# Scores of heads 4, 5, 8 and 9 as one float32 product instead of two FP32R products

## The chip, the cores and the metric

One NeuronCore of a Trainium2 chip runs the whole program. The metric is device time in microseconds of one execution, the median over several runs; a profile records one execution in full.

## The reference

Sparse attention, then two dense stages. Shapes: 2 batches, 8 heads, sequence 768, head dimension 64; so there are 16 heads in all, counted 0 to 15 below (head i is head i mod 8 of batch i div 8).

```
scores = q @ k.T / 8                      # per batch and head, 768 x 768
keep   = (key < 8) or (0 <= query - key < 96)
scores = where(keep, scores - slope[h] * distance, -1e9)
a      = softmax(scores); attn = a @ v    # slope[h] = 2 ** -(h + 1)
x      = attn, heads side by side         # 2 x 768 x 512
theta  = x @ w_theta
u      = x + w_tok_r @ (x * cos(theta)) + w_tok_i @ (x * sin(theta))
x2     = u + relu(u @ w_ch)
h      = relu(x2 @ w_in); c = conv3(h); out = (h * sigmoid(c)) @ w_out
```

All tensors are float32, the weights of the dense stages float64 bits that the kernel converts.

## The kernel before, in words

**Row tiles and steps.** A head is cut into six tiles of 128 query rows. Each tile needs only 232 key columns (96 before it, the 8 global ones, its own 128; tile 0 only its own 128). Two tiles are one step: step j = 3i + tp is part tp (0, 1, 2) of head i, and `run_fast` (L879) is one loop over all 48 steps and the lags behind them. In step j it emits, in this order: the scores of step j (`scores`, L353), the row minima of step j-1 on VectorE (`softmax`, L380), the exponentials of j-2 on ScalarE (`exps`, L395), the transposes of j-3 on TensorE (`transposes`, L402), their copy from PSUM of j-4 on ScalarE (`evacuate`, L412), the product with V of j-5 (`pv`, L416), and for every third step the normalisation of a head on VectorE (`normalise`, L291). The order of this loop is the order of each engine's instructions; there is no other scheduler.

**Scores.** The step's PSUM bank first takes a bias product (the "table" against a scaled identity, `eye`, written by POOL in `slope`, L333); heads 10 and later drop that product in their second and third step and add the bias on VectorE instead (`fused`, L344). Then come the tiles' products, L377. There are two ways:
- *Split*, heads 2 to 15: float32 is split into a high part in FP32R and a low rest. K holds the high part of the keys on partitions 0 to 63 and the low part on 64 to 127; Q is there twice, so that one FP32R product gives q_high * (k_high + k_low) and a second one q_low * (k_high + k_low). The parts are made in `split` (L264): query high by ScalarE (L306, `"  A"`), query low by VectorE (L310, `"   V"`), key low by VectorE (L90, `" V"`). The high key part is loaded directly by a POOL DMA (`keys`, L261) into K of buffer i mod 2, which it can enter only when the scores of head i-2 have been computed. Queries (128 x 768) and the keys' lower copy (64 x 816) come by two SP DMAs into a staging buffer (`load`, L249).
- *Whole*, heads 0 and 1: one float32 product of unsplit operands, L367. Queries of head 0 stand on partitions 0 to 63 of `scratch`, those of head 1 on 64 to 127 of the first columns of `xs[1]`, zeros on the other half; the keys of both heads stand one above the other in `scratch`, so that the zeros leave out the other head's keys. The queries are scaled in place by ScalarE.

For head i+1 the split is emitted during head i: query high in its first step, the two low parts in its second, followed by `load(i + 3)`; `keys(i + 2)` stands in the third step of head i, `load_v(i + 1)` too.

**Between the heads.** When two heads of a batch are done, their 128 columns of x are transposed (`transpose_x`, L526) in two groups of three on TensorE (tile X, a single PSUM bank), one group in the first and one in the second step of heads 4, 6, 8 and so on; ScalarE copies each group out (tile xT), the first copy in the same step as the second group. `split_xT` (L537) on VectorE follows in the next head. The theta products of batch 0 run from about head 11 on among the steps.

**The conveyor.** The float64 weights are converted piece by piece by `Net.conveyor` (L148): per piece six steps, `magnitude` (ScalarE, L98), three bit operations on VectorE (L102, L106, L110; the last frees the staging buffer and lets SP load the next piece), the high part (ScalarE, L82) and the low part (VectorE, L90). `net.run(k)` (L183) makes k steps of it; the last line of the loop says how many per step. Twelve pieces belong to this stage; what is left of them is finished after the loop (`tail`, L748).

Of the kernel before, what the change touches and what calls it, by code (L numbers as in the profile page):

```python
# [19 lines left out]
B, H, S, D = 2, 8, 768, 64  # L20
DM, DFF = H * D, 1024
P = 128
# [3 lines left out]
NH = B * H  # L26
# [10 lines left out]
STAGE = S + NT * KW  # L37
# [3 lines left out]
TURN = 6.283185  # L41
TWO32 = float(2.0 ** 32)
FUSED = 10
LAG_SM, LAG_EXP, LAG_T, LAG_EV, LAG_PV, LAG_N = 1, 2, 3, 4, 5, 6


# [178 lines left out]
class Attention:  # L225
# [21 lines left out]
        self.xs = xs  # L247

    def load(self, i, whole=False):  # L249
        if i < NH:  # L250
            b, h = divmod(i, H)
            src, st = self.net.io["qk"][b, :, h, :], self.st[i % 2]
            if whole:
                self.nc.sync.dma_start(st, src)
            else:
                self.nc.sync.dma_start(st[:, 0:S], src[:, 0:S])
                self.nc.sync.dma_start(st[D:P, S:STAGE], src[D:P, S:STAGE])

    def keys(self, i):
        if i < NH:  # L260
            b, h = divmod(i, H)  # L261
            self.nc.gpsimd.dma_start(self.K(i), self.net.io["qk"][b, :, h, S:STAGE])

# [39 lines left out]
def scaled(net, eh, el, q, hi, lo):  # L303
    nc = net.nc
    if eh == "A":
        nc.scalar.activation(hi, q, AF.Copy, scale=QSCALE)  # L306
    elif eh == "V":
        nc.vector.tensor_scalar(hi, q, QSCALE, None, op0=ALU.mult)
    if el == "V":
        nc.vector.scalar_tensor_tensor(lo, q, QSCALE, hi.bitcast(F32), op0=ALU.mult, op1=ALU.subtract)  # L310


class FastAttention(Attention):
# [6 lines left out]
        self.o = {}  # L320
        self.whole = [net.head["scratch"][:, 0:S], xs[1].rearrange("p t d -> p (t d)")[:, 0:S]]

    def second(self):

        nc, q = self.nc, self.whole[1]
        nc.sync.dma_start(q[D:P], self.net.io["qk"][0, D:P, 1, 0:S])
        nc.gpsimd.memset(q[0:D], 0.0)

    def eye(self, i):
        h = i % H  # L330
# [7 lines left out]
    def spread(self, i):  # L338

        if FUSED <= i < NH:  # L340
            T = self.net.head["table"][:, RW:].bitcast(F32)
            self.nc.gpsimd.tensor_scalar(self.bias[i % 2], T, 2.0 ** -(i % H + 1), None, op0=ALU.mult)

    def fused(self, j):  # L344
        return j % 3 > 0 and j // 3 >= FUSED

# [6 lines left out]
    def scores(self, j):  # L353

        i, tp = divmod(j, 3)
        net = self.net
        Q, K, T = self.Q(i), self.K(i), net.head["table"]
        sp = net.bank("TH", 1) if tp == 2 and i < NH // 2 + 2 else net.bank("S", 2)
        f = self.fused(j)
        if tp == 0:  # L360
            net.mm(sp[:, 0 : 2 * RW], self.eye(i), T, True, False)
        elif not f:
            net.mm(
                sp[:, 0 : 2 * RW].rearrange("p (u c) -> p u c", u=2), self.eye(i),
                T[:, RW:].unsqueeze(1).to_broadcast([P, 2, RW]), True, False,
            )
        if i < 2:  # L367
            Q, K = self.whole[i].unsqueeze(1), net.head["scratch"][:, S:STAGE]
        A = Q.shape[1]
        for u in range(2):  # L370
            t = 2 * tp + u
            if t == 0:
                o, r = sp[:, PG:RW], K[:, 0:P]
            else:
                o, r = sp[:, RW * u : RW * u + RW], K[:, KW * (t - 1) + SKIP : KW * t + P]
            for a in range(A):
                net.mm(o, Q[:, a, t * P : t * P + P], r, f and a == 0, a == 1 if f else u + a == A)  # L377
        self.state[j] = {"sp": sp}
# [100 lines left out]
class Mix:  # L479
# [46 lines left out]
    def transpose_x(self, b, c, e="AA", second="X"):  # L526

        n = self.net
        for hf in range(2):
            xb = n.bank(second, 2) if hf and second != "X" else n.bank("X")  # L530
            for jj in range(3):
                t = 3 * hf + jj
                self.nc.tensor.transpose(xb[:, P * jj : P * jj + P], self.xs[b][:, t, P * c : P * c + P], n.head["ident"])
            yield
            n.hi(e[hf], self.xT[b][:, c, HALF * hf : HALF * hf + HALF], xb[:, 0:HALF])
# [343 lines left out]
def run_fast(tc, net):  # L879
    nc, io = net.nc, net.io  # L880
    xs = [net.slot(f"xs{b}", [P, NT, DM], F32, "xs") for b in range(2)]
    att = FastAttention(net, xs)
    mix = Mix(net, xs)
    att.slope(0)
    att.second()
    att.keys(2)
    att.load_v(0)
    att.load(2)
    att.load_v(1)
    att.load(3)  # L890
    mix.begin()
    mix.alloc_xTs()
    NJ = 3 * NH
    OPEN = {
        NJ + 2: ((0, (0, 1)),), NJ + 3: ((1, (0, 1)),), NJ + 4: ((2, (0, 1)),),
        NJ + 6: ((0, (2,)), (1, (2,)), (2, (2,)), (3, (0, 1, 2))),
    }
    first, last, splits, theta0 = Pipe(), Pipe(), deque(), None

    def theta_0():  # L900
        for t in range(NT):
            tiles = mix.theta(t, "TH", 1)
            for k in range(2):
                for _ in range(6):
                    th = next(tiles)
                yield
            first.add(later(mix.reduce_theta(th, mix.r[:, t])))

    def later(g):
        next(g)  # L910
        yield
        yield
        next(g, None)

    early = mix.trig0()

    def split(b, c):
        for _ in range(3 if (b, c) in ((0, 3), (1, 2)) else 5):
            yield
        splits.append((b, c))  # L920

    for j in range(NJ + LAG_N + 3):
        i, tp = divmod(j, 3)
        if j < NJ:
            att.scores(j)
        first.step()
        if 0 <= j - LAG_SM < NJ:
            att.softmax(j - LAG_SM)
        if tp == 1 and i + 1 < NH and (i + 1 < 3 or (i + 1) % H > 2):
            att.slope(i + 1)  # L930
        if tp == 1:
            att.spread(i + 1)
        if 0 <= j - LAG_EXP < NJ:
            att.exps(j - LAG_EXP)
        if 0 <= j - LAG_T < NJ:
            att.transposes(j - LAG_T)
        if 0 <= j - LAG_EV < NJ:
            att.evacuate(j - LAG_EV)
        if 0 <= j - LAG_PV < NJ:
            att.pv(j - LAG_PV)  # L940
        jj = j - LAG_N
        if 0 <= jj < NJ and jj % 3 == 2:
            att.normalise(jj // 3, att.o.pop(jj // 3))
        if j == 0:
            scaled(net, "A", None, att.whole[1][D:P], att.whole[1][D:P], None)
        if tp == 2:
            if i != 1:
                att.keys(i + 2 if i else 3)
        elif i > 0 and tp == 0:
            att.split(i + 1, "  A")  # L950
        elif i > 0:
            att.split(i + 1, "   V")
            att.split(i + 1, " V")
            att.load(i + 3)
        if i > 0 and tp == 2 and i + 1 < NH:
            att.load_v(i + 1)
        last.step()
        jj = j - LAG_N - 1
        if jj == NJ - 1:
            for chain in (mix.transpose_x(1, KC - 1, "AV", "O"), mix.split_xT(1, KC - 1, "V")):  # L960
                for _ in chain:
                    pass
        elif 0 <= jj < NJ and jj % 6 == 5:
            bc = divmod(jj // 6, KC)
            last.add(mix.transpose_x(*bc), split(*bc))
        if splits and (splits[0][0] == 0 or theta0 == "done"):
            b, c = splits.popleft()
            last.add(mix.split_xT(b, c, "V"))
            if (b, c) == (0, KC - 1):
                theta0 = theta_0()  # L970
        elif theta0 and theta0 != "done" and next(theta0, last) is last:
            theta0 = "done"
            mix.alloc_xTs()
        for t, cs in OPEN.get(j, ()):
            mix.theta1(t, cs)
        if NJ + 4 <= j <= NJ + 6:
            next(early, None)
        if j == 3:
            net.fetch()
        if 6 < j < NJ + 3:  # L980
            net.run(2 if j >= NJ else (3, 2, 3)[tp] if i > 10 else (2, 1, 1)[tp] if i % 2 else (1, 0, 1)[tp])
    last.drain()
    mix.tail(early)

# [44 lines left out]
def build(nc, io):  # L1029
    with tile.TileContext(nc) as tc, tc.tile_pool(name="const", bufs=1) as small:  # L1030
        head = {}
        net = Net(tc, io, small, None, None, head)
        with tc.tile_pool(name="idle", bufs=1, space=bass.MemoryType.PSUM) as ps, tc.manual_schedule():
            begin(nc, io, net, small, head, ps.tile([P, 512], F32, name="idle"))
        rv = nc.values_load(
            head["flag"][:1, :1], min_val=0, max_val=1, skip_runtime_bounds_check_because="it is the product of comparisons, 0 or 1"
        )
        with tc.If(rv == 1) as cmp:
            arm(tc, io, head, run_fast)
        with cmp.Else():  # L1040
            arm(tc, io, head, run_general)
# [95 lines left out]
```

## Time and profile before

| what | value |
|---|---|
| median of 3 runs | 424.14 us (423.72 to 425.51) |
| the profiled execution | 422.92 us, span 421.0 us |
| TensorE busy | 405.9 us, 96% |
| VectorE busy | 332.9 us, 79% |
| ScalarE busy | 223.9 us, 53% |
| GpSimd (POOL) busy | 23.8 us, 6% |
| read from memory, written | 42.99 MB, 3.15 MB |

The span is the time from the first to the last instruction of the profiled execution; the execution's own time holds some 2 us more around it. In the rows below PE is TensorE, PEld its weight loads, DVE VectorE, ACT ScalarE, POOL GpSimd, SP the queue that issues most DMAs. A row of a timeline gives the start, the duration, the engine, the line, the operation, output and inputs by name, shapes and count, and in brackets the idle time before it with what ended it. A matmul's end is modelled, so the distance between two starts says more than a duration. A float32 product shows as two matmul records, an FP32R product as one.

### The profile page before, as it was taken

The numbers are of one execution on the slowest core, as the hardware profiler recorded it, in microseconds if no ns is written. First come the engines' busy times: TensorE is split into PE (matmuls) and PEld (weight loads), VectorE is DVE, ScalarE is ACT, GpSimd is POOL, SyncE is SP. The second block draws the span as 40 slices with busy tenths as digits, with TensorE's granted clock in tenths as the row PEclk, the third lists the DMA queues.
The fourth block names the chain that finished last, engine by engine and source line by source line (L and its number), as shares of the span: only waits on it lengthen the run. The fifth ranks groups of instructions, "written<-read, shape, count | busy, mean of one in ns | idle before, by whom it ended". The sixth has DMA issues, their size and how long they took to land.

```text
span 421.0 us, 6542 instructions
## 1 busy us (share of the span) xinstructions
PE 405.9 (96%) x2418; PEld 379.4 (90%) x2418; DVE 332.9 (79%) x619; ACT 223.9 (53%) x443; POOL 23.8 (6%) x45
## 2 busy tenths in 40 slices
PE   8979989999999999999999999999999999999994
PEld 4969879889998899999999999999999998888884
DVE  5768989999868985999989999999999999800000
ACT  4749667868778875824535336455645546200000
POOL 5011103121200000000000000000000000000000
PEclk9998999999999999999999999999999999999999
DMA  5998788786410034025466553131000000110111
GB/s 171 318 259 277 184 256 243 214 224 177 143 39 1 2 113 112 2 75 181 123 198 200 154 149 100 52 100 51 2 0 2 0 0 2 60 54 36 50 51 58
DMA packets 17130, 46.66 MB, mean 111 GB/s; under 512 B 2304, under 2 KB 2752, under 8 KB 17088
## 3 DMA queue, kind: packets, MB, share of 16 engines
q1 hardware_dynamic: 14768, 40.10, 32.2%
q0 software_dynamic: 2016, 5.85, 4.9%
q8 instruction: 21, 0.34, 0.4%
q10 hardware_dynamic: 304, 0.20, 0.2%
q14 instruction: 21, 0.17, 0.1%
HBM read 42.99 MB, written 3.15 MB: 110 GB/s over the span
## 4 chain that ended last, share of the span: by engine, by line
PE 68%; DMA 12%; ACT 8%; DVE 7%; issue 4%; SPq 1%; POOL 0%; DVEq 0%; POOLq 0%; ACTq 0%
PE S L93 17%; PE O L93 17%; PE PT L93 14%; PE TH L93 11%; DMA qk<-qk 8%; PE X L93 7%; DMA a<-qk 2%; DMA wst<-w_tok 1%; DVE qk L90 1%; PE PT L409 1%; ACT a L400 1%; ACT z L82 1%; ACT qk L306 1%; ACT scratch L588 1%; DVE z L90 1%
## 5 line engine op out<-in xcount | busy, mean ns | idle before, releaser
L98 ACT ACTIVATE wbit<-wst 128x512 f32<-128x512 f32 (+1 forms) x38 | 23.4, 617 | 17.5 <-DMA wst<-w_tok 5.9
L93 PE MATMUL O<-a,a 128*128 128x65 f32 x236 | 30.7, 272 | 0.0
L93 PEld LDWEIGHTS O<-a,a 128*128 128x128 f32 x236 | 29.8, 196 | 0.2
L400 ACT ACTIVATE a<-S,nm 128x232 f32<-128x232 f32 (+1 forms) x52 | 19.7, 438 | 16.8 <-DVE rs L296 13.6
L82 ACT ACTIVATE a<-PT 128x512 f32<-128x512 f32 (+1 forms) x48 | 27.5, 572 | 1.2 <-PE PT L409 1.1
L409 PE MATMUL PT<-ident,a 128*128 128x128 f32 x176 | 27.1, 272 | 0.0
L93 PE MATMUL O<-wt,z 128*128 128x384 f32 x144 | 26.9, 334 | 0.0
L93 PE MATMUL TH<-wth,xTs 128*128 128x512 f32 x96 | 26.4, 409 | 0.3 <-ACT scratch L577 0.3
L93 PEld LDWEIGHTS S<-qk 128*128 128x128 f32 x136 | 20.2, 194 | 6.5 <-DVE qk L90 4.2
L93 PE MATMUL PT<-wt,z 128*128 128x384 f32 x132 | 25.8, 335 | 0.0
L93 PE MATMUL S<-qk 128*128 128x232 f32 (+1 forms) x136 | 21.9, 284 | 3.5 <-DVE qk L90 3.4
L93 PEld LDWEIGHTS O<-wt,z 128*128 128x128 f32 x144 | 25.2, 188 | 0.1
L110 DVE SCALAR_TENSOR_TENSOR wbit<-wst,wbit 128x512 int32<-128x512 int32 (+1 forms) x38 | 23.9, 630 | 1.2
L106 DVE SCALAR_TENSOR_TENSOR wbit<-wst,wbit 128x512 int32<-128x512 int32 (+1 forms) x38 | 24.2, 636 | 0.9
L82 ACT ACTIVATE wt<-wbit 128x384 fp32r<-128x384 f32 x24 | 12.6, 526 | 22.0 <-DVE wbit L110 13.5
L93 PEld LDWEIGHTS PT<-wt,z 128*128 128x128 f32 x132 | 23.2, 188 | 0.0
L93 PE MATMUL S<-wt,z 128*128 128x384 f32 x120 | 22.3, 336 | 0.1
L93 PEld LDWEIGHTS S<-wt,z 128*128 128x128 f32 x120 | 20.9, 188 | 0.4 <-ACT scratch L577 0.4
L90 DVE TENSOR_TENSOR qk<-a,qk 64x816 fp32r<-64x816 f32 x14 | 14.1, 1005 | 9.1 <-DMA qk<-qk 8.8
L102 DVE TENSOR_SCALAR wbit<-wbit 128x512 int32<-128x512 int32 (+1 forms) x48 | 18.7, 390 | 3.1 <-ACT wbit L98 3.0
L93 PEld LDWEIGHTS TH<-wth,xTs 128*128 128x128 f32 x96 | 16.9, 189 | 3.9 <-ACT scratch L577 0.5
L409 PEld LDWEIGHTS PT<-ident,a 128*128 128x128 f32 x176 | 19.9, 141 | 0.2
(224 smaller groups left out, 992.5 us busy)
## 6 DMA issues: line engine op xcount, KB each, us to landing
wst<-w_tok SPq DMA_DIRECT2D x18, 384.0 KB, 3.7
a<-v SPq DMA_DIRECT2D x16, 357.5 KB, 5.6
qk<-qk POOLq DMA_DIRECT2D x14, 408.0 KB, 5.7
a<-qk SPq DMA_DIRECT2D x14, 384.0 KB, 3.9
wst<-w_out SPq DMA_DIRECT2D x8, 512.0 KB, 3.6
a<-qk SPq DMA_DIRECT2D x14, 204.0 KB, 5.5
out<-scratch SPq DMA_DIRECT2D x11, 256.0 KB, 2.0
wst<-w_in SPq DMA_DIRECT2D x5, 512.0 KB, 4.0
```

Of the source, the lines that this page charges most:

```text
L82: self.nc.scalar.activation(out, in_, AF.Copy)
L90: e.tensor_tensor(out, in_, hi.bitcast(F32), op=ALU.subtract)
L93: self.nc.tensor.matmul(out, l, r, start=start, stop=stop)
L98: self.nc.scalar.activation(t.bitcast(F32), w[:, 1 : w.shape[1] : 2].bitcast(F32), AF.Copy, scale=REBIAS)
L102: self.nc.vector.tensor_scalar(t, t, 3, None, op0=ALU.logical_shift_left)
L106: self.nc.vector.scalar_tensor_tensor(t, w[:, 0 : w.shape[1] : 2], 29, t, op0=ALU.logical_shift_right, op1=ALU.bitwise_or)
L110: self.nc.vector.scalar_tensor_tensor(t, w[:, 1 : w.shape[1] : 2], -(1 << 31), t, op0=ALU.bitwise_and, op1=ALU.bitwise_or)
L306: nc.scalar.activation(hi, q, AF.Copy, scale=QSCALE)
L400: self.nc.scalar.activation(sS[:, c], x[:, c], AF.Exp, bias=s["nm"][:, u : u + 1], scale=-1.0)
L409: self.nc.tensor.transpose(pt[:, c], sS[:, self.columns(u, a)], net.head["ident"])
L588: nc.scalar.activation(a, a, AF.Sin, bias=n.head["half_pi"], scale=-TURN)
```

## The change

`WHOLE` names the heads that are computed whole: 0, 1, 4, 5, 8 and 9. For these `load`, `keys` and `split` do nothing. `pair(i)`, for i = 4 and 8, brings the queries and keys of heads i and i+1 on SP: queries of head i, the keys of both, queries of head i+1, into the same places that heads 0 and 1 used; it is emitted in the second step of head i-2, after `load`. `scale(i)` scales a query on ScalarE in the second step of the head before. Heads 0 and 1 keep their loads and zeros; head 1's scaling moves from step 0 to step 1. The conveyor's step counts per step of the loop change: from 2, 1, 1 (odd heads) and 1, 0, 1 (even heads) to 2, 2, 2 in heads 3, 4, 7 and 8 and 1, 0, 1 in the other heads up to 10; 3, 2, 3 in heads 11 to 15 stay; the 2 in each of the three steps past the last head go.

```diff
@@ -41,6 +41,7 @@
 TURN = 6.283185
 TWO32 = float(2.0 ** 32)
 FUSED = 10
+WHOLE = (0, 1, 4, 5, 8, 9)
 LAG_SM, LAG_EXP, LAG_T, LAG_EV, LAG_PV, LAG_N = 1, 2, 3, 4, 5, 6
 
 
@@ -247,7 +248,7 @@
         self.xs = xs
 
     def load(self, i, whole=False):
-        if i < NH:
+        if whole or (i < NH and i not in WHOLE):
             b, h = divmod(i, H)
             src, st = self.net.io["qk"][b, :, h, :], self.st[i % 2]
             if whole:
@@ -257,7 +258,7 @@
                 self.nc.sync.dma_start(st[D:P, S:STAGE], src[D:P, S:STAGE])
 
     def keys(self, i):
-        if i < NH:
+        if i < NH and i not in WHOLE:
             b, h = divmod(i, H)
             self.nc.gpsimd.dma_start(self.K(i), self.net.io["qk"][b, :, h, S:STAGE])
 
@@ -320,11 +321,26 @@
         self.o = {}
         self.whole = [net.head["scratch"][:, 0:S], xs[1].rearrange("p t d -> p (t d)")[:, 0:S]]
 
-    def second(self):
-
-        nc, q = self.nc, self.whole[1]
-        nc.sync.dma_start(q[D:P], self.net.io["qk"][0, D:P, 1, 0:S])
-        nc.gpsimd.memset(q[0:D], 0.0)
+    def half(self, i):
+        return slice(D * (i % 2), D * (i % 2) + D)
+
+    def query(self, i):
+        b, h = divmod(i, H)
+        r = self.half(i)
+        self.nc.sync.dma_start(self.whole[i % 2][r], self.net.io["qk"][b, r, h, 0:S])
+
+    def pair(self, i):
+
+        self.query(i)
+        for x in (i, i + 1):
+            b, h = divmod(x, H)
+            r = self.half(x)
+            self.nc.sync.dma_start(self.net.head["scratch"][r, S:STAGE], self.net.io["qk"][b, r, h, S:STAGE])
+        self.query(i + 1)
+
+    def scale(self, i):
+        q = self.whole[i % 2][self.half(i)]
+        scaled(self.net, "A", None, q, q, None)
 
     def eye(self, i):
         h = i % H
@@ -364,8 +380,8 @@
                 sp[:, 0 : 2 * RW].rearrange("p (u c) -> p u c", u=2), self.eye(i),
                 T[:, RW:].unsqueeze(1).to_broadcast([P, 2, RW]), True, False,
             )
-        if i < 2:
-            Q, K = self.whole[i].unsqueeze(1), net.head["scratch"][:, S:STAGE]
+        if i in WHOLE:
+            Q, K = self.whole[i % 2].unsqueeze(1), net.head["scratch"][:, S:STAGE]
         A = Q.shape[1]
         for u in range(2):
             t = 2 * tp + u
@@ -882,7 +898,8 @@
     att = FastAttention(net, xs)
     mix = Mix(net, xs)
     att.slope(0)
-    att.second()
+    att.query(1)
+    nc.gpsimd.memset(att.whole[1][0:D], 0.0)
     att.keys(2)
     att.load_v(0)
     att.load(2)
@@ -941,17 +958,21 @@
         jj = j - LAG_N
         if 0 <= jj < NJ and jj % 3 == 2:
             att.normalise(jj // 3, att.o.pop(jj // 3))
-        if j == 0:
-            scaled(net, "A", None, att.whole[1][D:P], att.whole[1][D:P], None)
         if tp == 2:
             if i != 1:
                 att.keys(i + 2 if i else 3)
-        elif i > 0 and tp == 0:
-            att.split(i + 1, "  A")
-        elif i > 0:
-            att.split(i + 1, "   V")
-            att.split(i + 1, " V")
+        elif i > 0 and i + 1 not in WHOLE:
+            if tp == 0:
+                att.split(i + 1, "  A")
+            else:
+                att.split(i + 1, "   V")
+                att.split(i + 1, " V")
+        elif tp == 1 and i + 1 in WHOLE:
+            att.scale(i + 1)
+        if tp == 1 and i > 0:
             att.load(i + 3)
+            if i + 2 in WHOLE and i % 2 == 0:
+                att.pair(i + 2)
         if i > 0 and tp == 2 and i + 1 < NH:
             att.load_v(i + 1)
         last.step()
@@ -977,8 +998,8 @@
             next(early, None)
         if j == 3:
             net.fetch()
-        if 6 < j < NJ + 3:
-            net.run(2 if j >= NJ else (3, 2, 3)[tp] if i > 10 else (2, 1, 1)[tp] if i % 2 else (1, 0, 1)[tp])
+        if 6 < j < NJ:
+            net.run((3, 2, 3)[tp] if i > 10 else 2 if i in (3, 4, 7, 8) else (1, 0, 1)[tp])
     last.drain()
     mix.tail(early)
 
```

## Rows read from the trace of the kernel before

**Rows 1.** Page: busy us, share of the span, instructions.

```profile
PE 405.9 (96%) x2418; PEld 379.4 (90%) x2418; DVE 332.9 (79%) x619; ACT 223.9 (53%) x443; POOL 23.8 (6%) x45
```

**Rows 2.** Stretches by engine: heads 3, 4, 6, 8, 10, then heads 3 to 10.

```profile
21.16:26.79 5.63, 5.63 (x50) 5.57 (x50) 3.88 (x9) 4.92 (x12) 1.09 (x3) 1.00 1.14 289
26.79:37.74 10.95, 8.07 (x56) 7.71 (x56) 8.29 (x16) 6.30 (x16) 1.10 (x3) 0.84 0.77 236
43.37:51.19 7.82, 6.83 (x56) 6.27 (x56) 7.62 (x15) 5.66 (x14) 1.26 (x3) 1.00 0.67 165
56.82:65.20 8.38, 6.88 (x56) 6.27 (x56) 8.18 (x15) 5.66 (x14) 0.54 (x2) 1.00 0.69 188
70.83:78.64 7.81, 6.56 (x54) 5.93 (x54) 7.46 (x18) 5.91 (x15) 2.00 (x4) 1.00 0.79 214
21.16:78.64 57.48, 50.86 (x408) 48.41 (x408) 48.42 (x91) 41.60 (x99) 9.02 (x16) 0.97 0.84 238
```

**Rows 3.** Timeline of TensorE, head 4: start us, us, instructions, idle before.

```profile
30.12 0.71 PE L93 MATMUL S<-qk 128*128 128x128 f32 x4 [2.88 <-DVE qk L90]
...
35.72 0.50 PE L533 MATMUL X<-ident,xs 128*128 128x128 f32 x3
35.98 0.46 PE L93 MATMUL TH<-table,qk 128*128 128x464 f32 x1
```

**Rows 4.** Timeline of TensorE, heads 0, 1 and 2: scores and what follows.

```profile
8.54 0.95 PE L93 MATMUL S<-scratch 128*128 128x232 f32 x4
9.15 0.54 PE L93 MATMUL TH<-table,qk 128*128 128x464 f32 x1
...
10.52 0.78 PE L93 MATMUL S<-scratch,xs 128*128 128x128 f32 x4
11.14 0.49 PE L409 MATMUL PT<-ident,a 128*128 128x128 f32 x3
...
11.68 0.95 PE L93 MATMUL S<-scratch,xs 128*128 128x232 f32 x4
12.46 0.60 PE L409 MATMUL PT<-ident,a 128*128 128x128 f32 x4
...
15.82 0.60 PE L93 MATMUL S<-qk 128*128 128x128 f32 x4
16.26 0.49 PE L409 MATMUL PT<-ident,a 128*128 128x128 f32 x3
...
17.40 0.46 PE L93 MATMUL S<-table,qk 128*128 128x464 f32 x1
17.69 0.62 PE L93 MATMUL S<-qk 128*128 128x232 f32 x4
18.15 0.60 PE L409 MATMUL PT<-ident,a 128*128 128x128 f32 x4
```

**Rows 5.** Waits of TensorE, 10 to 135 us: total, times, longest.

```profile
PE S L93 <- DVE qk L90: 3.4, 2, 2.9
PE X L533 <- ACT xT L82: 2.8, 4, 0.9
```

**Rows 6.** Chain that ended last, 15 to 80 us: start us, us, what.

```profile
20.60 8.44 DMA qk<-qk
...
37.18 5.51 DMA qk<-qk
```

**Rows 7.** Timeline of VectorE, 8 to 48 us.

```profile
23.03 0.69 DVE L106 SCALAR_TENSOR_TENSOR wbit<-wst,wbit 128x512 int32<-128x512 int32 x1
...
24.19 0.95 DVE L310 SCALAR_TENSOR_TENSOR qk<-a,qk 128x768 fp32r<-128x768 f32 x1
29.06 1.00 DVE L90 TENSOR_TENSOR qk<-a,qk 64x816 fp32r<-64x816 f32 x1 [3.92 <-DMA qk<-qk]
```

**Rows 8.** Timeline of ScalarE, 8 to 48 us.

```profile
22.90 0.85 ACT L306 ACTIVATE qk<-a 128x768 fp32r<-128x768 f32 x1 [0.29 <-DMA a<-qk]
...
31.44 0.80 ACT L400 ACTIVATE a<-S,nm 128x232 f32<-128x232 f32 x2 [4.98 <-DVE rs L296]
```

## The prediction

> **What bounds the kernel now.** I read the busy shares, then busy time head by head, then the waits, the chain that ended last, and the timelines around the waits. TensorE is busy 96% of the span [rows 1], so only what TensorE waits for, or is given to do, can move the end. There are two kinds of head. Head 3 takes 5.63 us with TensorE busy throughout, and heads 2, 5, 7 and 9 take the same within 0.01 us. The even heads, which also carry two groups of X transposes, take 10.95 (head 4), 7.82 (6), 8.38 (8) and 7.81 us (10) [rows 2]. A group of X transposes costs 0.26 us where nothing waits (35.72 to 35.98 [rows 3]), so heads 4, 6 and 8 should take about 6.2 us. Head 10 leaves out two bias products of 0.29 us (17.40 to 17.69 [rows 4]), so 5.6 us. The excess is 4.75 + 1.6 + 2.2 + 2.2 = 10.75 us. TensorE's listed idle time from head 3 to head 10 is only 57.48 - 50.86 = 6.6 us [rows 2]; the rest hides in matmul ends, which are modelled, and in head 4's clock: granted 0.84 on average, that is a stretch at 1.2 instead of 2.4 GHz right after the stall.
>
> The waits name two causes: scores that wait for VectorE's qk (longest 2.9 us, at head 4), and X transposes that wait for ScalarE's xT (4 times, up to 0.9 us) [rows 5]. The chain shows them to be one. Head 4's keys are issued at 20.60 us, when head 2 has left their buffer, and land 8.44 us later [rows 6]; VectorE, which has waited 3.92 us for them, subtracts for 1.00 us [rows 7]; TensorE starts head 4's scores right behind, at 30.12 us, after 2.88 us idle [rows 3]. The same link stands in the chain at heads 6, 8 and 10 (5.51 us of transfer for head 6 [rows 6]). 5.5 + 1.0 us from the end of head i's scores to the start of head i+2's does not fit into the 5.63 us of the head between. VectorE works in order: its wait also delays the row minima queued behind the subtraction, so ScalarE's exponentials, so the xT copies on which the X transposes wait.
>
> **The change part by part.**
>
> *Scores.* For heads 4, 5, 8 and 9 two FP32R products per row tile become one float32 product; both show as two matmul records, so the counts are equal. Head 1 already runs so. From its scores to the next operation it is 0.62 us in a head's first step and 0.78 in the second; head 2 takes 0.44 and 0.46 [rows 4]. The third step is like the second, and the bias product grows by 0.01: 0.18 + 0.33 + 0.33, about +0.85 us per head, **+3.4 us** in all, on the path since TensorE is full there. The lower bound is head 0, where a bias product and no transposes follow: 0.61 us (8.54 to 9.15 [rows 4]), 0.15 more per full step, +1.3 us in all. Here transposes follow, as in head 1, so I take 3.4.
>
> The Trainium skill ("FP8 and Floating Point Precision", TensorE Precision Notes) says that true FP32 makes four passes through the array, which speaks against this change. An estimate by that rule, with one pass for each FP32R product, is 1,288 columns per head times two extra passes at 2.4 GHz: 1.07 us per head, 4.3 us in all, and a sum of -4.7 us for the -5.6 below. Head 1's rows agree with the four passes; it is the split pair of head 2 that stays above its own ideal, so the rows show less extra.
>
> *Conversions.* VectorE loses 0.95 + 1.00 us in each of four heads, 7.8 us [rows 7]. ScalarE's 0.85 us over 128 partitions [rows 8] becomes one over 64, for which I take no gain; but it moves from the first to the second step of the head before, behind that step's evacuation and ahead of the xT copy. Head 1's scaling moves from step 0 to step 1; no other ScalarE work of the loop lies between, so 0.
>
> *Transfers.* A head brought in 128 x 768 queries and 64 x 816 keys on SP and 128 x 816 keys on POOL, 996 KB; it now brings 64 x 768 and 64 x 816, 396 KB, on SP. Four POOL issues go, and with them the loop through the keys' buffer for heads 4 to 11: the buffers of heads 6, 7, 10 and 11 were last read by heads 2, 3, 6 and 7, so their keys can start about two heads earlier. POOL keeps its order; ahead of keys(6) and keys(7) stand only eye products, which wait for scores two heads back. On SP the loads for heads 4 and 5, which waited for VectorE, go; load_v(2) and pair(4) move up behind the first weights. q4 waits for head 0's scores (done by 10.5 us), the two key halves for head 1's (about 14.5). If they land as late as head 4's keys did, 8.44 us, that is 23 us at most for the keys; ScalarE came to q4's place at 22.9 us [rows 8], and head 4's scores are due at 26.8. Behind pair(4) on SP stand load_v(3) and load(6), which are used a head or more later, and the weights' loads, which wait for VectorE as before. pair(8) is issued when head 5's scores end, a whole head before ScalarE scales q8 in head 7. So 0.
>
> *Weights.* The conveyor makes 6 steps each in heads 3, 4, 7 and 8 and 2 each in 5, 6, 9 and 10: 32 for 24. Six steps are one weight; four of them are VectorE's, at up to 0.69 us [rows 7], some 2.4 us a weight. Eight steps cost it 3.3 us against the 7.8 freed. From head 3 to head 10 it was busy 48.4 of 57.5 us [rows 2]; it will be 44 of 52. The load is uneven, since heads 5, 7 and 9 also split xT: there VectorE may hold more than TensorE's 5.6 to 6.5 us. I put 0.5 us for that (0 to 1.5). The six steps past the last head go; TensorE is full there, so 0.
>
> *What is late next.* An X group still needs its predecessor's xT copy, in heads 4 and 8 now behind a 0.85 us scaling. TensorE's step there grows by 0.33 us, which covers part of it: 0.4 us each, and 0.2 in heads 6 and 10, so 1.2 us (bounds 0, and the 2.8 us of [rows 5]).
>
> Sum: -10.75 + 3.4 + 0.5 + 1.2 = **-5.6 us**. The profiled execution took 422.92 us with a span of 421.0; this makes 417.3 and a span of 415.4. The median of the runs lies 1.2 us above that execution, so I predict 418.5 us. By the bounds, -10.75 + 1.3 is -9.4, and -10.75 + 3.4 + 1.5 + 2.8 is -3.05: 414.7 to 421.1 us.
>
> **The rivals.** A change of 0.5% (2.1 us) is about what a measurement of this kernel can tell from none.
>
> *Only head 4's stall goes.* The delays in heads 6 to 10 could be ScalarE's own, with exponentials, evacuations, scaling and weight steps in one queue. Then 4.75 us go and 3.4 come: -1.35, 422.8 us. For it: TensorE's idle time is booked to ScalarE's xT 4 times [rows 5]. Against it: before head 4's second step ScalarE itself stood still 4.98 us for VectorE [rows 8], which waited for the keys; the same order holds before heads 6, 8 and 10.
>
> *The wait moves to the pair's loads.* ScalarE works in order, so a scaling that waits for its query holds the exponentials and evacuations behind it. It decides once q4 lands after 22.9 us or the keys after 26.8. To end slower by 2.1 us it must bring 7.7 us of new stall, 3.9 at each of heads 4 and 8; priced at head 4's present excess, 4.75 each, it gives -5.6 + 9.5 = +3.9, 428.0 us. Against it stand the 3 us of slack of the keys and the 600 KB fewer per head.
>
> *More is gained.* If the X waits vanish and the products cost what head 0 shows: -9.4, 414.7 us.
>
> *The change does not do what it says*: keys(6) and keys(10) could still be held by an older instruction on POOL or reach their buffer no earlier. Heads 6 and 10 would keep their excess, 3.8 less the 0.4 already counted: -5.6 + 3.4 = -2.2, 421.9 us.
>
> **How the numbers follow.** Forecast (-3 to -7.5 us): 0.65. More: 0.08. POOL still holds keys: 0.06, half of it faster. Only head 4's stall goes: 0.13. Pair late: 0.08. So faster 0.76, same 0.16, slower 0.08. The range reaches from a little beyond the forecast, 416.0, to the second case, 422.8, which leaves out about 2 in 10.
>
> **What the profile would show.** Right: head 4 begins at about 26.8 us without an idle row, the granted clock stays at 1.00 from 10 us on, heads 4 and 8 take 7.1 to 7.7 us, heads 5 and 9 about 6.5, head 6 at most 6.6, head 10 at most 6.0; head 10 begins near 67 instead of 70.83 us. The float32 score groups take 0.62 and 0.78 us to the next operation. From 130 us on the work is the same, only earlier. Wrong: ScalarE idle until a transfer into scratch or xs lands, X groups still waiting 0.7 us and more, VectorE full in heads 5 to 9 with TensorE waiting for it, or score groups of 1 us and more.

## The result, and the profile after

The changed kernel takes 416.89 us (415.81 to 419.04, four runs) where the kernel before took 424.32 us beside it (423.72 to 425.51): a ratio of 0.9854, with a 95% interval of 0.981 to 0.9899. That is 7.4 us less by the medians and 6.2 by the ratio; 418.5 us was forecast, inside a range of 416.0 to 422.8. The profiled execution took 416.43 us with a span of 414.5, so 6.5 us less than the profiled execution before on both.

First the page, to be read against [rows 1]:

```profile
PE 404.9 (98%) x2418; PEld 380.0 (92%) x2418; DVE 325.6 (79%) x611; ACT 225.2 (54%) x443; POOL 22.3 (5%) x41
```

TensorE has as many matmuls as before and is busy 98% instead of 96%. VectorE has 8 instructions fewer (the two low parts of four heads), POOL 4 (the key loads of those heads).

Then the stretches of the changed kernel by head: head 3, 4, 5, 6, 7, 8, 9, 10, and heads 3 to 10 together (columns as in [rows 2]).

```profile
22.73:28.36 5.63, 5.63 (x51) 5.56 (x50) 4.81 (x11) 4.95 (x11) 1.09 (x2) 1.00 1.04 224
28.36:35.40 7.04, 7.04 (x57) 6.77 (x56) 5.53 (x12) 5.84 (x14) 1.32 (x3) 1.00 1.05 332
35.40:41.87 6.47, 6.47 (x50) 6.20 (x50) 5.21 (x10) 5.54 (x14) 0.52 (x1) 1.00 0.84 201
41.87:48.07 6.20, 6.20 (x56) 6.13 (x56) 6.07 (x11) 5.33 (x13) 0.56 (x1) 1.00 0.84 222
48.07:53.70 5.63, 5.63 (x51) 5.56 (x50) 4.99 (x12) 5.55 (x14) 1.38 (x3) 1.00 1.11 291
53.70:60.74 7.04, 7.04 (x57) 6.77 (x56) 6.57 (x13) 6.32 (x15) 2.45 (x3) 1.00 0.92 300
60.74:67.21 6.47, 6.47 (x51) 6.20 (x50) 4.96 (x10) 4.82 (x12) 0.00 (x0) 1.00 0.44 116
67.21:72.98 5.77, 5.77 (x54) 5.75 (x54) 5.64 (x14) 4.92 (x13) 0.56 (x1) 1.00 0.51 146
22.73:72.98 50.25, 50.25 (x408) 48.94 (x408) 43.77 (x87) 43.27 (x99) 7.89 (x11) 1.00 0.84 231
```

The second number, TensorE's busy time, equals the first in every row: from head 3 to head 10 TensorE is never idle, and its clock is at 2.4 GHz throughout. These heads take 50.25 us where they took 57.48. The price of the float32 products is read by comparing like with like: head 5 against head 7, 6.47 to 5.63, and head 4 against head 6, 7.04 to 6.20, both 0.84 us.

The keys now come early. In the timeline of POOL, the DMA issues of heads 6 and 10:

```profile
27.80 0.58 POOL L263 DMA_DIRECT2D qk<-qk  x1
...
47.51 0.58 POOL L263 DMA_DIRECT2D qk<-qk  x1 [6.58 <-PE TH L94]
```

Head 6 starts at 41.87 and head 10 at 67.21 us, so their keys are issued 14 and 20 us ahead, where it was 6.2 us before (for head 6, 37.18 us in [rows 6] against its start at 43.37 in [rows 2]).

One wait is new. In the changed kernel's waits of TensorE from 10 to 135 us (total, times, longest), only one is left that is longer than 0.3 us:

```profile
PE TH L94 <- ACT a L416: 1.9, 1, 1.9
```

It is the third step of head 1, at 14.98 us. ScalarE stood still there behind head 2's queries, which landed at 13.4 us instead of 11.8 (its timeline):

```profile
13.40 0.84 ACT L307 ACTIVATE qk<-a 128x768 fp32r<-128x768 f32 x1 [2.39 <-DMA a<-qk]
```

So head 2 starts at 17.10 instead of 15.52 us and head 3 at 22.73 instead of 21.16. The account of the span is: +1.57 in front of head 3, -7.23 in heads 3 to 10, and -0.84 behind them; head 11 takes 8.33 us, before 8.74, and the stretch from head 12's start to the end 333.2 us, before 333.6.

### The profile page after: what moved, and what is told of

It reads as the page before. It is cut to its first block, busy times and chain, and to the rows that moved or that the text cites. A ratio compares the mean times of both kernels' runs of the same rounds, so it can differ in the third digit from the quotient of the medians.

```text
span 414.5 us, 6520 instructions
## 1 busy us (share of the span) xinstructions
PE 404.9 (98%) x2418; PEld 380.0 (92%) x2418; DVE 325.6 (79%) x611; ACT 225.2 (54%) x443; POOL 22.3 (5%) x41
## 4 chain that ended last, share of the span: by engine, by line
PE 82%; ACT 5%; DMA 5%; DVE 5%; issue 1%; SPq 0%; DVEq 0%; ACTq 0%
PE O L94 22%; PE S L94 20%; PE PT L94 14%; PE TH L94 13%; PE X L94 7%; PE PT L425 4%; DMA a<-qk 2%; DMA wst<-w_tok 1%; DMA qk<-qk 1%; PE X L549 1%; ACT z L83 1%; ACT scratch L604 1%; DVE z L91 1%; ACT scratch L602 1%; DMA words<-n 1%
## 5 line engine op out<-in xcount | busy, mean ns | idle before, releaser
L407 DVE TENSOR_REDUCE nm<-S 128x2 f32<-128x464 f32 x26 | 16.6, 638 | 6.9 <-PE S L94 5.0
L94 PE MATMUL O<-x,win 128*128 128x384 f32 x96 | 17.4, 336 | 0.0
L94 PE MATMUL O<-wout,g 128*128 128x512 f32 x72 | 17.1, 390 | 0.0
```

The costliest lines, as they stand in the source:

```text
L94: self.nc.tensor.matmul(out, l, r, start=start, stop=stop)
L407: self.nc.vector.tensor_reduce(s["nm"], s["sp"][:, 0 : 2 * RW].rearrange("p (u c) -> p u c", u=2), axis=AX.X, op=ALU.min)
```

## The experiments

Two questions were open: whether the loop through the keys' buffer was the cause of the gain (and not the lighter VectorE, the fewer transfers or the moved conversions), and whether the new wait belongs to the change. Each time is compared with that of the kernel before, run beside it on the same chip; the runs come from three chips. `after_again` (the same kernel again), `v2_late` (the V load moved), `own_keys` (keys in a place of their own) and `old_steps` (the conveyor's steps) ran on the first; `before_new_steps` (the same edit the other way round), `first_pair` (one pair alone), `q2_first` (head 2's loads first) and `third_buffer` on the second; `before_q2_first`, `q2_q3_first` and `pair_and_buffer` (the mixture) on the third. Between chips the ratios are the better comparison.

### The same kernel again, and the V load moved

> The changed kernel once more, as the measure for the three runs beside it, and to see whether the new 1.9 us wait of head 1's third step (ScalarE behind head 2's queries, which landed at 13.4 us instead of 11.8) comes again. If it belongs to the change (the transfers that moved up ahead of it in time, the third V load above all), the wait is there again, over 1.5 us, and head 2 starts at about 17 us. If it was chance, head 2 starts near 15.5 us. Median near 417 us.

Measured: 417.88 us (415.79 to 419.47) against 423.63 before, ratio 0.9843 (0.9801 to 0.9885). The wait was there again, 1.88 us, as was expected if it belonged to the change; `before_new_steps` below decides otherwise. This time TensorE's clock also fell. The stretch from 15 to 18.5 us of this execution (columns as in [rows 2]; the granted clock is the third number from the end):

```profile
15.00:18.50 3.50, 3.48 (x13) 3.11 (x14) 2.56 (x4) 2.69 (x7) 0.00 (x0) 0.53 1.08 290
```

The same stretch of the changed kernel's first profiled execution:

```profile
15.00:18.50 3.50, 3.50 (x27) 3.38 (x27) 2.83 (x5) 2.86 (x8) 0.00 (x0) 1.00 1.06 257
```

The granted clock is 0.53, almost all of the stretch at 1.2 GHz, against 1.00. The idle time ahead of it is the same, 1.88 and 1.90 us; one execution does half the matmuls (13 against 27), and head 3 starts 1.7 us later.

Then the V load of head 2 moved:

```diff
             att.load(i + 3)
             if i + 2 in WHOLE and i % 2 == 0:
                 att.pair(i + 2)
-        if i > 0 and tp == 2 and i + 1 < NH:
+                if i == 2:
+                    att.load_v(2)
+        if i > 1 and tp == 2 and i + 1 < NH:
             att.load_v(i + 1)
```

> The changed kernel with the V load of head 2 emitted behind the pair's loads of heads 4 and 5, so that it is issued at about 17 us instead of 10.7. If the new wait in head 1 comes from that load sharing the DMA engines with head 2's queries, these land near 11.8 us again, head 2 starts about 1.5 us earlier and the time falls by 1 to 1.5 us against the changed kernel of the same call. If the wait is chance or comes from the queries' own place in the queue, nothing moves by more than 0.5 us.

Measured: 418.08 us (416.15 to 419.64), no faster than the changed kernel. In its profiled execution the wait was gone and head 2 started at 14.99 us, yet the runs gained nothing. The profile shows where it went: head 2 starts 2.1 us earlier than in the changed kernel's first profile and the span is only 0.2 us shorter, because heads 2 and 3 take 12.09 instead of 11.26 us and the stretch behind head 10 takes 342.6 instead of 341.5. So what the start gains can be lost elsewhere, and this median alone does not clear the V load. A later run settles it: the kernel `first_pair` below issues the V load early, at 10.84 us, as the change does, and had no such wait; `before_new_steps` below does not issue it before 17.16 us and had it. So the early V load is neither enough for the wait nor needed for it, and the cause named in the expectation falls.

### The keys in a place of their own, nothing else changed

```diff
+    def K(self, i):
+        if i in (4, 5, 8, 9):
+            x = NT * KW * (i % 2)
+            return self.spare[:, x : x + NT * KW]
+        return self.qk[i % 2][:, 2 * S :]
...
     mix.begin()
+    att.spare = mix.wt[0][1].rearrange("p a b c -> p (a b c)")
```

> The kernel before, with nothing changed but the place of the high keys of heads 4, 5, 8 and 9: they go to an idle FP32R tile instead of the buffer that heads 2, 3, 6 and 7 still read. All conversions, transfers and FP32R products stay. Theory (the loop through the keys' buffer set the pace, and the change gained by breaking it): the 10.75 us of excess in heads 4, 6, 8 and 10 go for the most part without the 3.4 us of float32 products; heads 3 to 10 take 48 to 51 us instead of 57.5, bounded by VectorE, which stays at 48 us busy there; median 413 to 418 us. Rival (the change gained by what it takes off VectorE and the DMA queues): VectorE and the transfers are as full as before, heads 3 to 10 stay at 55 us or more, median 421 us or more.

Measured: 417.85 us, ratio 0.9843 (0.9801 to 0.9884): the same as the changed kernel. Its heads 3 to 10:

```profile
24.76:73.72 48.96, 47.56 (x408) 46.55 (x408) 47.18 (x87) 40.77 (x96) 8.00 (x13) 1.00 0.96 261
```

Its waits of TensorE from 10 to 135 us, the first of them head 1's third step again:

```profile
PE TH L93 <- ACT a L406: 2.2, 1, 2.2
PE X L539 <- ACT xT L82: 1.8, 3, 0.9
```

48.96 us, although every head but 0 and 1 is still split, VectorE still does all its conversions (47.18 us busy, before 48.42) and all transfers remain. So the rival falls, and the loop through the buffer is what the change removed: opening it alone takes 8.5 us off these heads, the change 7.2. The float32 products are one way to open it, and what they save VectorE repays their price of 3.4 us only in part. In heads 4 to 7 they buy nothing: 23.64 us here, 25.34 in the changed kernel, 30.03 before. In heads 8 to 10 they buy a little: 19.69, 19.28 and 21.82 us. What they buy there is visible in the second row: with VectorE nearly full, X groups still wait 1.8 us, 1.3 of them in heads 8 and 10. ScalarE, which copies the groups out, waits 5.5 us for VectorE's `rs` between 25 and 75 us, in the changed kernel 0.5.

Heads 3 to 10 are 1.3 us shorter than in the changed kernel and the time is the same. In this profile the stretch behind head 10 takes 343.0 us, in the changed kernel's two 341.5 and 342.0; 1.1 us of it are two waits of TensorE, 0.66 us for VectorE at 82.33 us and 0.45 us for an X group's copy at 123.22.

### The conveyor's steps

```diff
-        if 6 < j < NJ:
-            net.run((3, 2, 3)[tp] if i > 10 else 2 if i in (3, 4, 7, 8) else (1, 0, 1)[tp])
+        if 6 < j < NJ + 3:
+            net.run(2 if j >= NJ else (3, 2, 3)[tp] if i > 10 else (2, 1, 1)[tp] if i % 2 else (1, 0, 1)[tp])
```

> The changed kernel with the conveyor's steps per loop step as before. Theory: TensorE is full in heads 3 to 10 either way, so those heads take 50.3 us within 0.5, and what the six steps behind the last head cost is at most the 0.45 us that an X group waited there: the time is within 0.7 us of the changed kernel. Rival (the new counts are what pays: less work for VectorE and ScalarE behind the last head): 2 us or more slower than the changed kernel, lost behind 115 us.

Measured: 418.21 us against 417.88 for the changed kernel. Heads 3 to 10 take 50.36 us. So the time is as the theory had it. An X group's wait returns behind them, 0.44 us at 122.86 us (0.45 at 127.54 in the kernel before), another of 0.61 us appears at 170.42, and head 11 takes 8.09 instead of 8.33 us. In the other direction, the new counts in the kernel before (the same edit, the other way round):

> The kernel before with the change's conveyor counts alone. Theory: the keys' loop still sets the pace, and eight more conveyor steps lie in heads 3 to 10; these heads take 57 to 61 us and the time is 0 to 4 us above the kernel before (424 to 428 us). Rival (moving the conversions forward is what gained): 421 us or less.

Measured: 424.74 against 424.12 us, ratio 1.0009 (0.9981 to 1.0038). Heads 3 to 10 take 58.98 us in its profile. Moving the conversions neither gains nor costs by itself; in the change they fill room that other edits made.

Its profile also answers the question of the start. This is a kernel with the keys, loads and order of the kernel before, and head 2's queries landed late all the same. ScalarE, from its timeline:

```profile
13.74 0.84 ACT L306 ACTIVATE qk<-a 128x768 fp32r<-128x768 f32 x1 [2.77 <-DMA a<-qk]
```

And TensorE behind it, from its own:

```profile
15.33 0.47 PE L93 MATMUL TH<-table,qk 128*128 128x464 f32 x1 [2.29 <-ACT a L400]
```

The wait therefore does not need the change.

### One pair alone

```diff
-WHOLE = (0, 1, 4, 5, 8, 9)
+WHOLE = (0, 1, 4, 5)
...
-            net.run((3, 2, 3)[tp] if i > 10 else 2 if i in (3, 4, 7, 8) else (1, 0, 1)[tp])
+            net.run((3, 2, 3)[tp] if i > 10 else 2 if i in (3, 4) else (2, 1, 1)[tp] if i % 2 else (1, 0, 1)[tp])
```

> The changed kernel with heads 8 and 9 split as before, so that only heads 4 and 5 are whole, and the conveyor's counts of before in heads 7 and 8. Theory: heads 4 to 7 take what they take in the changed kernel, 25.3 us, heads 8 to 10 what they took before, 21.8 us, since head 8's keys wait for head 6's scores again and head 10's for head 8's; heads 3 to 10 together 52.8 us, 2.5 us above the changed kernel, 419 to 421 us. Rival (one stall at the start was all): within 0.7 us of the changed kernel or faster, since two heads' float32 cost, 1.7 us, goes.

Measured: 418.56 us, ratio 0.9874 (0.9832 to 0.9916). Heads 4 to 7, then 8 to 10:

```profile
27.44:52.77 25.33, 25.33 (x206) 24.66 (x206) 21.78 (x39) 21.29 (x50) 3.11 (x6) 1.00 0.95 274
52.77:73.58 20.81, 18.83 (x157) 17.76 (x156) 19.40 (x39) 16.04 (x39) 3.94 (x6) 1.00 0.80 222
```

Heads 4 to 7 are exactly as in the changed kernel (7.04 + 6.47 + 6.20 + 5.63 = 25.34). In heads 8 to 10 TensorE waits 2.0 us again, and VectorE waits for the keys of heads 8 and 10, 1.28 us until 51.73 and 0.86 us until 65.09. Its waits from 25 to 75 us, a kind that neither the changed kernel nor `own_keys` has in that stretch:

```profile
DVE qk L91 <- DMA qk<-qk: 2.1, 2, 1.3
```

Not all of the 2.0 us is the loop's. In `pair_and_buffer` below these heads are split too, but the keys of heads 8 and 9 have a place of their own:

```profile
53.38:73.01 19.63, 18.41 (x157) 17.70 (x156) 19.17 (x39) 16.08 (x39) 2.15 (x4) 1.00 0.77 205
```

Opening the loop is worth 1.2 us there, and what whole heads take off VectorE is worth 0.35 us more than the products cost: 1.5 us in these profiles for the second pair (20.81 against 19.28). Heads 8 to 10 are 1.0 us shorter than expected (head 8 takes 7.44 us, where it was 8.38 in the kernel before), and the time came out 0.4 us below the expected band. Most of the gain lies in the first pair. The times alone do not decide against the rival, that the first pair does all of it: 418.56 lies 0.7 us above the 417.88 of the changed kernel on another chip, 1.3 by the ratios, and the intervals overlap. The profile does, since the rival would have put heads 8 to 10 below 19.3 us.

### The start: head 2's loads first

```diff
     att.keys(2)
+    att.load(2)
     att.load_v(0)
-    att.load(2)
```

> The changed kernel with the loads of head 2 emitted ahead of the first V load, which is 357 KB and moves behind them. Theory: head 1's third step waits for ScalarE, which stands behind head 2's queries; these land 1 us or more earlier, the 1.9 us wait falls below 0.9 us, TensorE's clock does not fall behind it, and the time is 1 to 3 us below the changed kernel: 414 to 416.5 us. Rival (the wait only moves, to the first product with V or to head 2's keys): no change, 416.5 to 418 us.

Measured: 414.81 us (414.48 to 417.29), ratio 0.9799 (0.9768 to 0.983), where the changed kernel had 417.88 us and 0.9843 on the first chip: 1.9 us less by the ratios, 3.1 by the medians, with intervals that overlap a little. ScalarE, in its timeline, no longer waits:

```profile
10.97 0.84 ACT L307 ACTIVATE qk<-a 128x768 fp32r<-128x768 f32 x1
```

Head 2 starts at 15.01 us and heads 3 to 10 take 50.25 us, as in the changed kernel. The same edit in the kernel before:

> The kernel before with head 2's loads ahead of the first V load, nothing else. Theory: the late landing of head 2's queries belongs to no kernel of the two but to the start of some executions, and this order cures it in both; but before the change the start's delay is partly covered, since head 4 waits for its keys anyway. The keys' loop stays: heads 3 to 10 take 55 to 58 us, 421.5 to 424 us. Rival (the changed kernel's gain was a matter of the start): 419 us or less.

Measured: 421.71 us, ratio 0.9965 (0.994 to 0.999). With the start put right in both kernels, the change is worth 0.9799 / 0.9965 = 0.983, or 7.1 us of 424 (by the two intervals, some 1.7 us either way), close to the 7.23 us that heads 3 to 10 show. Heads 3 to 10 took 58.83 us in its profile, 0.8 us above the expected band; that execution (424.79 us) was the longest of its runs.

The queries of head 3 as well (`load(3)` ahead of `load_v(1)`, on top of the last edit):

> The changed kernel with head 2's loads ahead of the first V load and head 3's ahead of the second. Theory: head 3's queries, for which ScalarE still waited 1.25 us in the kernel with head 2's loads first, land before they are wanted; TensorE's 0.2 us wait and the clustered start go: 0.3 to 1 us below that kernel, 414 to 414.6 us. Rival (the second V load is then late for head 1's products): 415.5 us or more.

Measured: 414.76 us (414.46 to 416.56), ratio 0.9815 (0.9777 to 0.9854), the same time as without it, though ScalarE's wait for head 3's queries is gone and head 3 starts at 20.57 instead of 21.01 us. Head 12, which waits 0.66 us for VectorE (0.53 without the edit), still starts 0.3 us earlier and the profiled span is 0.4 us shorter (412.8 against 413.2); the expected 0.3 to 1 us is too small for these runs to show.

### Versions that open the loop with fewer float32 products

A third buffer for the high keys and no whole heads beyond 0 and 1, on the kernel before, with head 2's loads first:

```diff
+    def K(self, i):
+        r = (i - 2) % 3 if i < 11 else (i - 11) % 2
+        return self.spare if r == 2 else self.qk[r][:, 2 * S :]
...
```

> The kernel before with a third buffer for the high keys (an idle FP32R tile), taken in turn by heads 2 to 10, and head 2's loads ahead of the first V load; all heads but 0 and 1 split, as before, and the conveyor as before. Theory: the loop through the keys' buffer is open as with the whole heads, without float32 products; heads 3 to 10 take 48 to 50 us, now with VectorE full and X groups waiting up to 2 us in all; head 2 starts at about 15 us; 412 to 416 us. Rival (without the fewer transfers and conversions of the change the start does not keep up): heads 3 to 5 wait for transfers, 418 us or more.

Measured: 415.48 us (415.22 to 415.63), ratio 0.9801 (0.9773 to 0.9829). Heads 3 to 10:

```profile
22.36:72.14 49.78, 47.76 (x409) 46.61 (x408) 48.36 (x91) 41.96 (x99) 9.04 (x15) 1.00 0.95 271
```

Of its waits of TensorE from 10 to 135 us, the X groups', three of the four in heads 4 to 10:

```profile
PE X L537 <- ACT xT L82: 2.4, 4, 0.9
```

TensorE has 2.5 us less to do than in the changed kernel and waits 2.0 of them away, for VectorE (48.36 of 49.78 us busy) by way of ScalarE. The loop can be opened by a buffer as well as by float32 products.

A mixture, heads 4 and 5 whole, heads 8 and 9 split with keys of their own (`first_pair`, `own_keys` for 8 and 9, head 2's loads first):

> Heads 4 and 5 whole as in the change, heads 8 and 9 split with their high keys in an idle FP32R tile, head 2's loads first. Theory: the keys' loop is open for both pairs; TensorE saves the 1.7 us of float32 products of heads 8 and 9, VectorE has room for their conversions there; heads 3 to 10 take 48.6 to 49.7 us and the time is 413.5 to 414.6 us. Rival (VectorE fills in heads 7 to 9 and X groups wait): 50 us or more for heads 3 to 10, 414.8 us or more.

Measured: 415.81 us (414.71 to 417.81), ratio 0.9821 (0.9782 to 0.9859). A miss, and both numbers lie where the rival had them: heads 3 to 10 took 51.96 us in its profiled execution, the longest of its runs. X groups waited 1.2 us in heads 8 to 10, as the rival says; 1.0 us went in front of head 5, to nothing that the profile names. That part stays open.

The fastest of all are the changed kernel with head 2's loads first, 414.81 us, and with head 3's first too, 414.76; they can't be told apart, nor, by its ratio of 0.9801, can the third buffer's 415.48 us.

## Why the prediction was right

**The bound** held. Opening the keys' loop and nothing else (`own_keys`) takes 8.5 of the 10.75 us of excess away, and in the change the excess goes entirely: TensorE's busy time equals the length of every head from 3 to 10, and 7.23 + 3.36 = 10.6 us came back. One point is finer than the prediction had it: some 2 of the 10.75 us do not go with the loop alone. As far as the profile lists them, they are X groups that wait while VectorE is nearly full (1.3 us in `own_keys`), and they go in the change because whole heads also take work off VectorE. The prediction's second number was needed. The listed idle time, 6.6 us, would have been too small; the excess over a head with no wait also counts the half clock after the stall and the waits under modelled matmul ends.

**The scores** cost 0.84 us a head against 0.85 predicted: 3.4 us in all, the term that was on the path. The timeline of TensorE shows it, here the scores of head 4's second step and what follows them:

```profile
30.98 0.94 PE L94 MATMUL S<-scratch 128*128 128x232 f32 x4
31.76 0.60 PE L425 MATMUL PT<-ident,a 128*128 128x128 f32 x4
```

0.78 us, as in head 1 [rows 4]. The lower bound from head 0 was rightly not taken, since transposes follow here as they do in head 1. The estimate by the Trainium skill's four passes ("FP8 and Floating Point Precision", TensorE Precision Notes), 1.07 us per head, is above the 0.84 measured here; the measurement decides.

**Transfers and conversions** were put at no cost on TensorE's path, and the head windows show none. VectorE was expected to be busy 44 of 52 us in heads 3 to 10; it is 43.77 of 50.25. The 0.5 us for its uneven load did not come: head 10 starts at 67.21 us (67 forecast) although head 4 started 1.6 us later than foreseen.

**Weights.** The six steps past the last head were put at 0, but where they stand an X group waits 0.44 to 0.45 us behind the last head (127.54 us before, 122.86 in `old_steps`), and where they are gone it does not. That wait is one of the 4 of [rows 5]; only 2.3 of the 2.8 us there lie in heads 4 to 10.

**What is late next** was over-sized: X groups were to wait 1.2 us and wait 0. VectorE no longer makes ScalarE late (ScalarE's waits for its `rs` fall from 13.6 us between 25 and 80 us to 0.5 between 25 and 75), so ScalarE runs ahead of TensorE, and the xT copies wait 2.1 us for X groups instead of the reverse. With the 0.5 us above, this is the 1.7 us by which heads 3 to 10 did better (-7.23 against -5.6).

**What was missed** is the start. The forecast had head 2 begin where it did in the profile of before. Head 1's third step waited 1.9 us in the changed kernel's profile, and the prediction priced no such thing; it also took the landing of head 2's queries for fixed, when it varies between executions of either kind of kernel. In the profiled pair it took back 1.6 of the 7.2 us. That -5.6 and the profile's -6.5 lie so near one another is therefore luck in part: 1.7 us forecast too little in heads 3 to 10 and 0.84 us behind them that were not forecast stand against 1.6 us lost at the start. No run ties the late start to either kernel; with the start put right in both, they differ by 7.1 us, 1.5 more than forecast and within the 1.7 us that this figure can be off. The mechanism was right, and the two small terms were too large.

Of the rivals, "only head 4's stall goes" falls with heads 8 and 10, which lose 1.3 and 2.0 us although head 8 carries a float32 cost of 0.84; "the wait moves to the pair's loads" is seen in small, 0.59 us of ScalarE's time before head 4's scaling, which TensorE never felt; "POOL still holds keys" is answered by the issue times above. "More is gained" is right about the X groups and wrong about the products. Among the signs, the granted clock was to stay at 1.00 from 10 us on; it did in this profile and not in that of `after_again`.

## What to carry to other kernels

Where a buffer is refilled only after its last reader, compare refill plus conversion with the work that lies between; if it does not fit, a further buffer or operands that need no conversion both open the loop, and here they gave the same time (414.81 and 415.48 us with head 2's loads first, ratios 0.9799 and 0.9801). Price a wait by the length of a stage that has none, not by the idle time listed: a stall in one engine's fixed order comes back as small waits elsewhere and, in some executions, as a lower clock of TensorE. Put the load that is needed first at the head of its queue: swapping two loads at the start gave 1.9 to 3.1 us in the changed kernel and 1.5 to 2.1 in the kernel before, between a fifth and two fifths of what the change itself did.

## What was not expected of the hardware

The same load, head 2's queries, issued at 6.4 to 6.5 us behind the first V load, was taken up by ScalarE at 10.95, 11.1, 11.8, 13.4, 13.4, 13.7, 13.8 and 14.0 us in eight profiled executions; what decides it is not settled. Ahead of the V load, issued at 5.8 us, it was always there by 10.97 us, in five. In the five executions where TensorE waited 1.88 us or more for it, the granted clock of the 3.5 us behind the wait was 0.53, 0.63 and 0.61 after 1.88, 2.23 and 2.50 us of idle time, but 1.00 after 1.90 and 2.29 us: the length of the wait does not sort them.
